# Eight raw weight tiles loaded into the empty ring of weights, and projections issued ahead of the sums of squares

## The chip, the cores and the metric

The kernel runs on one core of one Trainium2 chip. The metric is the device time of one execution in microseconds (us), the median of three runs. TensorE does the matmuls and loads their stationary operand ("weight load") by a part of its own; VectorE, ScalarE and GpSimd work on vectors, and SyncE issues the DMAs.

## The reference

Three stages follow one another, all in float32. Attention with random features (4 batches, 8 heads, 576 tokens, 64 numbers a head, 128 features):

```
phi(x) = exp(x_s @ omega.T - |x_s|^2/2 - max) / sqrt(128)     # x_s = x / 64**0.25
kv = phi(k).T @ v ;  z = sum of phi(k) over the tokens
attn = (phi(q) @ kv) / (phi(q) @ z + 1e-6)
```

Then a dense network on 2304 tokens of 512 numbers, `g = h if h > 0 else 0.01*h` with `h = x @ w_in` (512 x 2048) and `x1 = g @ w_out`; w_in and w_out come as 64-bit floats. Last, a gated network of eight experts: each token goes to the expert with the largest logit, through `relu(x1 @ w1[e]) @ w2[e]`, scaled by two gate values.

## The kernel before

The program is written in Python against a scheduler: it states operations in an order, and the scheduler lays them out in one fixed queue for each engine. An engine then runs its queue strictly in order and waits at an instruction until its operands and its destination are free.

**The opening.** The attention is cut into items of four 128-row tiles. A k item (27 of all) goes through the stages `s_load` (its inputs), `s_split` (squares of the inputs, line 270, on VectorE for the first three items, then on GpSimd), `s_proj` (the projection `pw` on omega, line 310, and the sums of squares `s2p`, line 288, as matmuls with `halves`), `s_phi` (the maximum `mx` on VectorE, line 322, then `ngm` and `bias`, lines 329 and 331, then four exponentials on ScalarE, line 339) and `s_kv` (the products `kvp` with v, line 379). A q item ends in transposes `qtp`, the product `nump` (line 441) and a transpose `xtp`, whose two halves `xh` and `xl` (line 216) are the input of the dense network. Thirteen items (k 0 to 7, the four of q that make the first 256 tokens, k 8) must be through before the first matmul `hp` of the dense network (lines 488 to 490), and three more begin before it; these sixteen take the sums of squares from TensorE (`by_pe`). `tick()` moves every open item one stage on.

In `project` the two matmuls for `s2p` stand ahead of those for `pw`, and VectorE copies `s2p` out of its bank at once (line 290).

**The weights.** `load_w` loads one half of a weight unit, 512 KB of 64-bit floats, into `wraw`, a ring of two tiles in the pool `wst`, and turns it into a pair of float32 tiles: ScalarE scales the upper word (line 205), VectorE puts the words together in three instructions (lines 206 to 208) into `w`, ScalarE copies to `wih` or `woh` (line 213) and GpSimd subtracts to `wil` or `wol` (line 216). Those pairs lie in `wring`, 32 tiles that the experts' weights use again later. Eight loads belong to the opening (`WPRE`), their order is `order`: w_in halves 0 and 1 of unit 0, w_out halves 0 and 1 of unit 0, then unit 1. A load is kept behind the newest input by `issue_after(newest[-1])`, and the third load waits until the first tile of the ring of two is free.

**The inputs.** The first nine k items come in three groups, `xgroup` and `vgroup`, loaded when the first item of a group begins; the others in pairs, `xpair`, a ring of three.

## Time and profile before

| | us |
|---|---|
| median of 3 runs | 829.49 |
| lowest, highest | 827.87, 835.15 |
| profiled execution, own time | 826.18 |
| its span, first to last instruction | 824.5 |
| TensorE busy in the span (matmul) | 805.0 (98%) |
| weight loads | 711.4 (86%) |
| VectorE, ScalarE, GpSimd | 438.6, 371.7, 152.0 |
| granted TensorE clock | 0.998 |

The profile is one execution. The page's slices show TensorE near full in all 40, and VectorE at 6 to 9 tenths in the first seven or so and at 3 to 6 later: the first tenth of the span is unlike the rest. Ends of matmuls are modelled, so that TensorE's gaps are better seen in the weight loads, whose idle time before each is listed with what ended it.

### The profile page before, as it was taken

How to read it: one execution, taken by the hardware profiler on the slowest of the kernel's cores; microseconds unless marked ns; L12 is line 12 of the kernel's file. 1: busy time of each engine (PE TensorE's matmuls, PEld its weight loads, DVE VectorE, ACT ScalarE, POOL GpSimd, SP SyncE). 2: the span in 40 equal slices, each digit the busy share in tenths (PEclk: the TensorE clock that was granted, in tenths of full speed). 3: DMA queues.
4: the chain of work that ended last, by engine and by line, in shares of the span. 5: the costliest groups of instructions: out<-in, count | busy, mean ns of one | idle time of the engine just before them, and what ended most of it. 6: DMA issues, size and time to landing. Idle time of an engine off the chain costs nothing. (4 is left out here: it accounts for less than half of the span.)

```text
span 824.5 us, 15807 instructions
## 1 busy us (share of the span) xinstructions
PE 805.0 (98%) x6037; PEld 711.4 (86%) x6037; DVE 438.6 (53%) x1118; ACT 371.7 (45%) x1238; POOL 152.0 (18%) x172
## 2 busy tenths in 40 slices
PE   9999999999999999999999999999999999999996
PEld 6777777788899898989898898888889989999994
DVE  6988779836644645634653544545644444343220
ACT  4887767625566236545425243122423434332210
POOL 3513324400211011121010010031004221130101
PEclk9999999999999999999999999999999999999999
DMA  6746655402342111152021000036306554150101
GB/s 217 217 126 178 197 172 166 151 8 71 81 84 73 45 20 52 58 71 64 26 32 21 2 26 1 27 110 102 78 28 209 165 167 144 56 162 27 45 14 35
DMA packets 45153, 72.74 MB, mean 88 GB/s; under 512 B 5905, under 2 KB 27665, under 8 KB 45074
## 3 DMA queue, kind: packets, MB, share of 16 engines
q1 hardware_dynamic: 41554, 62.22, 27.6%
q0 software_dynamic: 3520, 9.47, 3.7%
q8 instruction: 49, 0.80, 0.4%
q14 instruction: 30, 0.25, 0.1%
HBM read 61.08 MB, written 10.59 MB: 87 GB/s over the span
## 5 line engine op out<-in xcount | busy, mean ns | idle before, releaser
L488 PE MATMUL hp<-xh,wih 128*128 128x256 f32 x576 | 163.2, 283 | 0.9 <-ACT g L493 0.5
L490 PE MATMUL hp<-xh,wil 128*128 128x256 f32 x576 | 161.6, 281 | 2.3 <-POOL wil L216 2.2
L489 PE MATMUL hp<-xl,wih 128*128 128x256 f32 x576 | 161.6, 281 | 0.6 <-DVE xl L216 0.6
L508 PE MATMUL acc<-woh,gh 128*128 128x512 f32 x288 | 117.4, 408 | 0.8 <-ACT gh L213 0.8
L510 PE MATMUL acc<-woh,gl 128*128 128x512 f32 x288 | 114.7, 399 | 0.3 <-DVE gl L216 0.3
L509 PE MATMUL acc<-wol,gh 128*128 128x512 f32 x288 | 114.7, 398 | 0.0
L488 PEld LDWEIGHTS hp<-xh,wih 128*128 128x128 f32 x576 | 108.1, 188 | 3.8 <-ACT g L493 0.8
L490 PEld LDWEIGHTS hp<-xh,wil 128*128 128x128 f32 x576 | 108.1, 188 | 3.5 <-POOL wil L216 3.4
L489 PEld LDWEIGHTS hp<-xl,wih 128*128 128x128 f32 x576 | 108.1, 188 | 3.1 <-DVE xl L216 1.0
L495 DVE SCALAR_TENSOR_TENSOR g<-hp,g 128x512 f32<-128x512 f32 x56 | 38.6, 690 | 113.5 <-ACT g L493 113.0
L339 ACT ACTIVATE h<-pw,bias 128x128 f32<-128x128 f32 x288 | 84.9, 370 | 25.1 <-DVE bias L331 18.3
L493 ACT COPY g<-hp 128x512 f32<-128x512 f32 x72 | 42.2, 586 | 113.3 <-PE hp L490 113.3
L776 PE MATMUL eht<-exh,ewh 128*128 128x256 f32 (+1 forms) x256 | 76.5, 299 | 0.0
L778 PE MATMUL eht<-exh,ewl 128*128 128x256 f32 (+1 forms) x256 | 75.5, 295 | 0.0
L777 PE MATMUL eht<-exl,ewh 128*128 128x256 f32 (+1 forms) x256 | 75.4, 295 | 0.0
L281 ACT ACTIVATE nat<-nat 128x64 f32<-128x64 f32 x224 | 55.5, 257 | 40.6 <-DVE bias L331 27.8
L779 ACT ACTIVATE ehh<-eht 128x256 fp32r<-128x256 f32 (+1 forms) x64 | 26.4, 412 | 91.5 <-PE eht L778 91.3
L510 PEld LDWEIGHTS acc<-woh,gl 128*128 128x128 f32 x288 | 54.0, 188 | 13.1 <-DVE gl L216 1.0
L508 PEld LDWEIGHTS acc<-woh,gh 128*128 128x128 f32 x288 | 54.1, 188 | 11.5 <-ACT gh L213 1.6
L322 DVE TENSOR_REDUCE mx<-pw 128x4 f32<-128x512 f32 x66 | 45.2, 684 | 32.9 <-PE pw L305 22.2
L509 PEld LDWEIGHTS acc<-wol,gh 128*128 128x128 f32 x288 | 54.1, 188 | 9.6
L216 POOL TENSOR_TENSOR rawl<-xpair,rawh 128x256 fp32r<-128x256 f32 x38 | 29.4, 773 | 162.5 <-ACT rawh L213 153.6
(176 smaller groups left out, 1636.5 us busy)
## 6 DMA issues: line engine op xcount, KB each, us to landing
eraw<-w SPq DMA_DIRECT2D x32, 512.0 KB, 3.7
wraw<-w_in SPq DMA_DIRECT2D x16, 512.0 KB, 3.9
wraw<-w_out SPq DMA_DIRECT2D x16, 512.0 KB, 3.7
x_d<-rows SPq DMA_DIRECT2D x9, 514.0 KB, 3.4
xpair<-qT SPq DMA_DIRECT2D x18, 256.0 KB, 3.1
nat<-k_nat SPq DMA_DIRECT2D x27, 128.0 KB, 3.0
xpair<-kT SPq DMA_DIRECT2D x12, 256.0 KB, 2.7
nat<-q_nat SPq DMA_DIRECT2D x23, 128.0 KB, 2.2
```

The source lines that it names most:

```text
L281: nc.scalar.activation(nat[:, j], nat[:, j], AF.Square, scale=math.sqrt(sc * sc / 2.0), accum_out=s2[:, j:j + 1])
L322: nc.vector.tensor_reduce(o, pj.rearrange("p (j h) m -> p j h m", h=2), axis=AX.X, op=ALU.max)
L339: st["e_last"] = nc.scalar.activation(h[:, j, :], src[:, j // 2, j % 2], AF.Exp, bias=bias[:, j:j + 1], scale=sc).ins
L488: nc.tensor.matmul(hp[:, i, :], a, xh[:, d, :], start=d == 0, stop=False)
L489: nc.tensor.matmul(hp[:, i, :], a, xl[:, d, :], start=False, stop=False)
L490: nc.tensor.matmul(hp[:, i, :], b_, xh[:, d, :], start=False, stop=d == ND - 1)
L508: nc.tensor.matmul(acc[t], a, h_, start=u == 0 and i == 0, stop=False)
L509: nc.tensor.matmul(acc[t], a, l_, start=False, stop=False)
L510: nc.tensor.matmul(acc[t], b_, h_, start=False, stop=u == NU - 1 and i == 1)
L776: nc.tensor.matmul(t, wh, self.xh[:, d, 0:n], start=d == 0, stop=False)
L777: nc.tensor.matmul(t, wh, self.xl[:, d, 0:n], start=False, stop=False)
L778: nc.tensor.matmul(t, wl, self.xh[:, d, 0:n], start=False, stop=d == ND - 1)
```

## The change

Eight tiles of the still empty `wring` serve as raw tiles for the eight loads of the opening, so that none of these waits for the ring of two. The three k groups are loaded first, in one go (`k_group`), then two raw tiles, and each further raw tile after a `load_w` (`ahead`); in the opening they are no longer tied behind the newest input. In `project` the projections now stand ahead of the sums of squares, `s2p` stays in its bank, and VectorE copies it in `phi`, behind the maximum. The squares `sq` get a third place (the tag `g`). All other work is the same: each engine has as many instructions of each kind as before, and the queues are equal again from about the 1,050th of TensorE's 5,751 instructions on.

```diff
+        spare = [wring.tile([P, 512, 2], I32, name="wraw", tag="w") for _ in range(WPRE)]
+        raws = {}
+
+        def raw_of(kind, u, half, raw):
+            with ExitStack() as order_:
+                if dense[0]:
+                    order_.enter_context(tc.issue_after(newest[-1]))
+                if kind == "in":
+                    nc.sync.dma_start(raw.rearrange("p (i a) b -> p i (a b)", i=2),
+                                      w_in[2 * half * P:2 * (half + 1) * P, u * 256:(u + 1) * 256].bitcast(I32).rearrange("(i p) a -> p i a", i=2))
+                else:
+                    f = 2 * u + half
+                    nc.sync.dma_start(raw.rearrange("p a b -> p (a b)"), w_out[f * P:(f + 1) * P, :].bitcast(I32))
+            return raw
...
-            raw = pool.tile([P, 512, 2], I32, name="wraw", tag="wraw")
+            if (kind, u, half) not in raws:
+                raws[kind, u, half] = raw_of(kind, u, half, pool.tile([P, 512, 2], I32, name="wraw", tag="wraw"))
+            raw = raws.pop((kind, u, half))
...
-                with tc.issue_after(newest[-1]):
...
+        def fetch(dst, src):
+            newest.append(nc.sync.dma_start(dst, src).ins)
+
+        def group_of(src, at, grp):
 
             first, m, big = grp
-            if at == first:
+            if (src.tensor.name, first) not in groups:
...
-                sq = sb.tile([P, 2 * P], F32, name="sq", tag="gl")
+                sq = sb.tile([P, 2 * P], F32, name="sq", tag="g" if st["turn"] % 3 == 2 else "gl", bufs=1 if st["turn"] % 3 == 2 else 2)
...
         def project(st, nt):
-            if st["by_pe"]:
-                s2 = ps_h.tile([P, 2, 2], F32, name="s2p", tag="h")
-                for j in range(2):
-                    nc.tensor.matmul(s2[:, j, :], st["sq"][:, j * P:(j + 1) * P], halves, start=True, stop=True)
-                s2s = att.tile([P, 4], F32, name="s2", tag="s2")
-                nc.vector.tensor_copy(s2s.rearrange("p (h j) -> p j h", h=2), s2)
-                st["s2"] = s2s
...
             st["pj"] = pj
+            if st["by_pe"]:
+                s2 = ps_h.tile([P, 2, 2], F32, name="s2p", tag="h")
+                for j in range(2):
+                    nc.tensor.matmul(s2[:, j, :], st["sq"][:, j * P:(j + 1) * P], halves, start=True, stop=True)
+                st["s2"] = s2
...
             s2 = st["s2"]
+            if st["by_pe"]:
+                s2 = att.tile([P, 4], F32, name="s2", tag="s2")
+                nc.vector.tensor_copy(s2.rearrange("p (h j) -> p j h", h=2), st["s2"])
...
+        def k_group(first, m):
+            group_of(kT, first, (first, m, True))
+            vs = sb.tile([P, 1024], F32, name="vgroup", tag="xl", bufs=3)
+            vs = vs[:, 0:m * 5 * HV].rearrange("p (m n) -> p m n", m=m)
+            fetch(vs, v_nat[first:first + m].rearrange("m p n -> p m n"))
+            groups["v", first] = vs
...
+        def ahead():
+            if spare:
+                o = order[WPRE - len(spare)]
+                raws[o] = raw_of(*o, spare.pop(0))
+
+        for at in range(0, 9, 3):
+            k_group(at, 3)
+        ahead()
+        ahead()
         for i in range(first + LEAD):
             tick(seq.pop(0) if i < first + NEW else None)
             while loaded < min(WPRE, (i - WFROM) * WPRE // (first + LEAD - WFROM)):
                 load_w(*order[loaded], wst)
                 loaded += 1
+                ahead()
 
 
         tabv = tab_d.rearrange("(c n) o -> c (n o)", n=SLOT)
```

TensorE's queue at the first k items, before. `s2p` are the sums of squares, `pw` the projections, `kvp` the products with v:

```order
L288 MATMUL s2p<-halves,sq 128x2 x2
L310 MATMUL pw<-om_raw,xgroup 128x256 x2
L288 MATMUL s2p<-halves,sq 128x2 x2
L310 MATMUL pw<-om_raw,xgroup 128x256 x2
L288 MATMUL s2p<-halves,sq 128x2 x2
L310 MATMUL pw<-om_raw,xgroup 128x256 x3
L379 MATMUL kvp<-vgroup,h 64x132 x2
L379 MATMUL kvp<-vgroup,h 64x66 x2
L310 MATMUL pw<-om_raw,xgroup 128x256
L379 MATMUL kvp<-vgroup,h 64x66 x4
L288 MATMUL s2p<-halves,sq 128x2 x2
L379 MATMUL kvp<-vgroup,h 64x66 x4
```

and after the change:

```order
L317 MATMUL pw<-om_raw,xgroup 128x256 x2
L322 MATMUL s2p<-halves,sq 128x2 x2
L317 MATMUL pw<-om_raw,xgroup 128x256 x2
L322 MATMUL s2p<-halves,sq 128x2 x2
L317 MATMUL pw<-om_raw,xgroup 128x256 x2
L322 MATMUL s2p<-halves,sq 128x2 x2
L317 MATMUL pw<-om_raw,xgroup 128x256
L396 MATMUL kvp<-vgroup,h 64x132 x2
L396 MATMUL kvp<-vgroup,h 64x66 x2
L317 MATMUL pw<-om_raw,xgroup 128x256
L396 MATMUL kvp<-vgroup,h 64x66 x4
L322 MATMUL s2p<-halves,sq 128x2 x2
```

The projection of an item now stands first, and the sums of squares come to lie between a projection and the products with v; the last item's first half of a projection still meets `kvp` directly.

VectorE's queue around the first weight conversion, before (`w_187` is the first converted tile, `mx` the maximum of one item):

```order
L322 TENSOR_REDUCE mx<-pw 128x2x2
L206 TENSOR_SCALAR w_187<-w_187 128x512
L290 COPY s_303<-s2p 128x2x2
L207 SCALAR_TENSOR_TENSOR w_187<-wraw,w_187 128x512
L329 SCALAR_TENSOR_TENSOR ngm<-mx,s_267 128x4
L322 TENSOR_REDUCE mx<-pw 128x2x2
L208 SCALAR_TENSOR_TENSOR w_187<-wraw,w_187 128x512
L206 TENSOR_SCALAR w_255<-w_255 128x512
L331 TENSOR_TENSOR bias<-ngm,s_267 128x4
```

and after (`w_197` is the first converted tile):

```order
L346 TENSOR_TENSOR bias<-ngm,s_354 128x4
L334 TENSOR_REDUCE mx<-pw 128x2x2
L217 TENSOR_SCALAR w_197<-w_197 128x512
L342 COPY s_387<-s2p 128x2x2
L218 SCALAR_TENSOR_TENSOR w_197<-wraw,w_197 128x512
L344 SCALAR_TENSOR_TENSOR ngm<-mx,s_387 128x4
L334 TENSOR_REDUCE mx<-pw 128x2x2
L219 SCALAR_TENSOR_TENSOR w_197<-wraw,w_197 128x512
L217 TENSOR_SCALAR w_264<-w_264 128x512
L346 TENSOR_TENSOR bias<-ngm,s_387 128x4
```

The first conversion stood behind the fifth `mx` and now stands behind the seventh, and the copy out of `s2p` stands behind the maximum of its item.

SyncE's queue of DMA issues, before, from the second k group on:

```order
L250 DMA xgroup<-kT 128x3x256
L352 DMA vgroup<-v_nat 128x3x330
L188 DMA wraw<-w_in 128x2x512 x2
L250 DMA xgroup<-kT 128x3x256
L352 DMA vgroup<-v_nat 128x3x330
L250 DMA xpair<-qT 128x2x256
L200 DMA wraw<-w_out 128x1024
L250 DMA xpair<-qT 128x2x256
L200 DMA wraw<-w_out 128x1024
L250 DMA xpair<-qT 128x2x256 x2
```

and after:

```order
L251 DMA xgroup<-kT 128x3x256
L251 DMA vgroup<-v_nat 128x3x330
L251 DMA xgroup<-kT 128x3x256
L251 DMA vgroup<-v_nat 128x3x330
L183 DMA wraw<-w_in 128x2x512 x2
L251 DMA xpair<-qT 128x2x256 x3
L251 DMA nat<-q_nat 128x256
L251 DMA nat<-k_nat 128x256
L381 DMA vb<-v_nat 128x330
L381 DMA vb<-v_nat 128x264
L187 DMA wraw<-w_out 128x1024 x2
```

The third k group and its v went ahead of the two w_in tiles, three pairs of q follow without a w_out load between them, and w_out comes behind those and small loads of later items.

## Rows read from the trace of the kernel before

**Rows 1.** Busy us per engine (x instructions), clock, DMA share, GB/s; two stages.

```profile
0.00:46.50 46.50, 43.79 (x380) 32.96 (x380) 36.28 (x109) 29.39 (x85) 19.05 (x32) 1.00 0.65 206
...
165.00:230.00 65.00, 64.41 (x502) 56.90 (x501) 35.02 (x114) 30.86 (x121) 8.20 (x10) 1.00 0.21 52
```

**Rows 2.** Timeline of weight loads: start, length, what, count, [idle before, releaser].

```profile
4.36 0.93 PEld L288 LDWEIGHTS s2p<-halves,sq 128*128 128x128 f32 x4 [0.54 <-PE warm L143]
...
6.72 0.73 PEld L310 LDWEIGHTS pw<-om_raw,xgroup 128*128 128x128 f32 x4
...
16.52 0.55 PEld L379 LDWEIGHTS kvp<-vgroup,h 128*64 128x64 f32 x16 [0.33 <-issue]
17.14 0.30 PEld L310 LDWEIGHTS pw<-om_raw,xgroup 128*128 128x128 f32 x2
17.46 0.63 PEld L288 LDWEIGHTS s2p<-halves,sq 128*128 128x128 f32 x4
18.01 0.30 PEld L310 LDWEIGHTS pw<-om_raw,xgroup 128*128 128x128 f32 x2
...
22.89 0.52 PEld L288 LDWEIGHTS s2p<-halves,sq 128*128 128x128 f32 x4
23.42 0.31 PEld L379 LDWEIGHTS kvp<-vgroup,h 128*64 128x64 f32 x8
```

**Rows 3.** Weight loads by group, 0 to 46.5 us: busy, mean ns, idle before.

```profile
L379 PEld LDWEIGHTS kvp<-vgroup,h 128*64 128x64 f32 x144 | 6.3, 136 | 3.7 <-ACT h L339 2.0 <-issue 1.0 <-ACT woh L213 0.3
...
L441 PEld LDWEIGHTS nump<-kv,et 128*64 128x64 f32 x64 | 2.2, 137 | 1.2 <-ACT et L430 0.3 <-ACT wih L213 0.3 <-ACT h L339 0.3
```

**Rows 4.** The same timeline of weight loads, later.

```profile
21.43 0.52 PEld L288 LDWEIGHTS s2p<-halves,sq 128*128 128x128 f32 x4 [0.45 <-POOL sq L270]
...
34.47 1.16 PEld L310 LDWEIGHTS pw<-om_raw,xpair 128*128 128x128 f32 x6 [1.23 <-DMA xpair<-kT]
...
49.94 0.19 PEld L489 LDWEIGHTS hp<-xl,wih 128*128 128x128 f32 x1 [1.02 <-DVE xl L216]
```

**Rows 5.** Timeline of VectorE (DVE), same columns.

```profile
6.59 0.69 DVE L322 TENSOR_REDUCE mx<-pw 128x4 f32<-128x512 f32 x1 [0.68 <-PE pw L310]
...
15.00 0.42 DVE L206 TENSOR_SCALAR w<-w 128x512 int32<-128x512 int32 x1
...
15.74 0.69 DVE L207 SCALAR_TENSOR_TENSOR w<-wraw,w 128x512 int32<-128x512 int32 x1
...
17.44 0.67 DVE L208 SCALAR_TENSOR_TENSOR w<-wraw,w 128x512 int32<-128x512 int32 x1
...
19.24 1.67 DVE L208 SCALAR_TENSOR_TENSOR w<-wraw,w 128x512 int32<-128x512 int32 x1
...
24.28 0.68 DVE L322 TENSOR_REDUCE mx<-pw 128x4 f32<-128x512 f32 x1
...
37.57 0.16 DVE L443 TENSOR_SCALAR rec<-nump 128x4 f32<-128x4 f32 x1 [1.25 <-PE nump L441]
...
49.48 0.41 DVE L216 TENSOR_TENSOR xl<-xtp,xh 128x256 fp32r<-128x256 f32 x1
```

**Rows 6.** Timeline of ScalarE (ACT).

```profile
8.98 3.21 ACT L339 ACTIVATE h<-pw,bias 128x128 f32<-128x128 f32 x12 [6.68 <-DVE ngm L329]
```

**Rows 7.** VectorE by group, 15 to 49.9 us: busy, mean ns, idle before.

```profile
L207 DVE SCALAR_TENSOR_TENSOR w<-wraw,w 128x512 int32<-128x512 int32 x8 | 7.3, 916 | 0.0
L208 DVE SCALAR_TENSOR_TENSOR w<-wraw,w 128x512 int32<-128x512 int32 x8 | 6.4, 802 | 0.0
```

**Rows 8.** Timeline of GpSimd (POOL).

```profile
18.85 1.50 POOL L216 TENSOR_TENSOR wil<-w,wih 128x512 fp32r<-128x512 f32 x1 [1.95 <-ACT wih L213]
```

**Rows 9.** Timeline of the DMA issues on SyncE.

```profile
18.19 0.34 SPq L200 DMA_DIRECT2D wraw<-w_out  x1
...
54.69 0.89 SPq L188 DMA_DIRECT2D wraw<-w_in  x2
```

**Rows 10.** Longest TensorE wait, 46 to 230 us: total, times, longest.

```profile
PE hp L490 <- POOL wil L216: 2.2, 3, 1.1
```

More of the change, by code (lines that the diff above doesn't have):

```diff
@@ L186, in load_w @@
                 wh, wl = win[u]
-                with tc.issue_after(newest[-1]):
-                    nc.sync.dma_start(raw.rearrange("p (i a) b -> p i (a b)", i=2),
-                                      w_in[2 * half * P:2 * (half + 1) * P, u * 256:(u + 1) * 256].bitcast(I32).rearrange("(i p) a -> p i a", i=2))
                 wh, wl = wh[:, 2 * half:2 * half + 2, :], wl[:, 2 * half:2 * half + 2, :]
@@ L197, in load_w @@
                 wh, wl = wout[u]
-                f = 2 * u + half
-                with tc.issue_after(newest[-1]):
-                    nc.sync.dma_start(raw.rearrange("p a b -> p (a b)"), w_out[f * P:(f + 1) * P, :].bitcast(I32))
                 wh, wl = wh[:, half, :], wl[:, half, :]
@@ L237, in xt_tiles @@
             return xT[c]
-        def group_of(st, src, at, grp):
+        def fetch(dst, src):
+            newest.append(nc.sync.dma_start(dst, src).ins)
+        def group_of(src, at, grp):
             first, m, big = grp
-            if at == first:
+            if (src.tensor.name, first) not in groups:
                 if big:
@@ L249, in group_of @@
                 for a, b in zip(cuts, cuts[1:]):
-                    newest.append(nc.sync.dma_start(t[:, a:b], src[at + a:at + b].rearrange("m p c -> p m c")).ins)
+                    fetch(t[:, a:b], src[at + a:at + b].rearrange("m p c -> p m c"))
                 groups[src.tensor.name, first] = t
@@ L255, in split_x @@
             st["turn"] = next(turns)
-            st["raw"] = group_of(st, src, at, grp)
+            st["raw"] = group_of(src, at, grp)
             st["tight"] = not both_done[0]
@@ L263, in split_x @@
                 st["nat"] = att.tile([P, 4, HD], F32, name="nat", tag="nat")
-                newest.append(nc.sync.dma_start(st["nat"][:, 0:nt, :], nat).ins)
+                fetch(st["nat"][:, 0:nt, :], nat)
         def squares(st, nt):
             if st["by_pe"]:
-                sq = sb.tile([P, 2 * P], F32, name="sq", tag="gl")
+                sq = sb.tile([P, 2 * P], F32, name="sq", tag="g" if st["turn"] % 3 == 2 else "gl", bufs=1 if st["turn"] % 3 == 2 else 2)
                 (nc.vector if st["turn"] < 3 else nc.gpsimd).tensor_mul(sq, st["raw"], st["raw"])
@@ L347, in s_load @@
             def s_load():
-                split_x(st, kT, 9 * b + g, grp, k_nat[b, g], 4)
-                if big and at == first:
-                    vs = sb.tile([P, 1024], F32, name="vgroup", tag="xl", bufs=3)
-                    vs = vs[:, 0:m * 5 * HV].rearrange("p (m n) -> p m n", m=m)
-                    nc.sync.dma_start(vs, v_nat[at:at + m].rearrange("m p n -> p m n"))
-                    groups["v", first] = vs
+                split_x(st, kT, at, grp, k_nat[b, g], 4)
             def s_split():
```

## The prediction, made before the changed kernel ran

> **What bounds the kernel now.** I read the stages first. From 165 us on TensorE is busy 64.41 of 65.00 us, and in the first 46.5 us 43.79 [rows 1]. The queues of before and after are the same from about TensorE's 1,050th instruction on, so all that the change can give or cost lies in the opening and the 100 us behind it. The next view is the timeline of weight loads, which shows TensorE's gaps better than the matmuls, whose ends are modelled. A float32 matmul is two instructions there: a whole projection is four loads.
>
> Three things are to be seen in it. First, TensorE really is close to full in the opening: behind the warm-up its first real load comes at 4.36 [rows 2], and most loads follow one another at once. Second, a gap of 0.33 us stands ahead of `kvp` behind a projection, and it is put down to "issue" (nothing that the profile shows) as well as to ScalarE [rows 2, 3]. Behind `s2p` there is none: 22.89 + 0.52 = 23.41, and `kvp` starts at 23.42 [rows 2]. A gap that has the same length whoever is named is not a wait for data; it goes with the pair of neighbours. Third, TensorE can't start the dense network fully before 49.94, where `hp` waits for `xl`, the last half of the fourth q item, which VectorE writes at 49.48 [rows 4, 5].
>
> So two engines share the opening: TensorE, and from 15.00, when the first conversion starts, VectorE, whose queue ends in that `xl`. What VectorE does there I read from its timeline. The longest hole in it behind 15.00 is 1.25 us at 37.57, where it waits for TensorE's `nump` [rows 5].
>
> **The change, part by part.** Nothing is added to or taken from any engine's count. The extra raw tiles cost no instruction. They take places 0 to 7 of the ring of 32; the weights of units 0 to 5 take the next 24, and those of units 6 and 7 take the eight raw places again, long after their conversion. Cost: 0. The work that hides their allocation is the same 24 pairs' conversion; were it late, unit 6 would wait for it.
>
> *Projection first.* Before, the first maximum waits until 6.59 for a projection that stood behind `s2p` [rows 5]. Now the projection's loads begin at 4.36. One `s2p` is 18.01 - 17.46 = 0.55 [rows 2], so `mx` moves to about 5.8 to 6.0. ScalarE's first exponentials at 8.98 [rows 6] follow; since `bias` still stands behind the second `mx`, I take 0.6 of those 0.8 for TensorE's first `kvp`.
>
> *Fewer gaps.* All gaps ahead of `kvp` and `nump` in the opening come to 3.7 + 1.2 = 4.9 us [rows 3], which is about fourteen of 0.33. In the new queue I count seven places where `kvp` or `nump` still follows a projection or a transpose directly (three around the first three k items, four among the q items). Seven times 0.33 is 2.3 us saved.
>
> *Waits in the middle.* `s2p` waited 0.45 for squares from GpSimd, which had two places; with three and with squares ahead of the weight splits in its queue I count that as gone. A projection waited 1.23 for a pair from memory [rows 4]. That pair still needs a place in the ring of three, so the issue moves with the projection that frees it; I take half, 0.6.
>
> TensorE's own sum is 0.6 + 2.3 + 0.45 + 0.6 = 3.9 us. It is not the answer, because VectorE must follow.
>
> *VectorE.* The first conversion now stands behind the seventh `mx`. When is that? From the first load at 4.36: three rounds of projection and sums of squares of 0.75 + 0.55 each (the projection is 0.73 and a start-up of 0.02 [rows 2]) end at 8.26. Half a projection ahead of `kvp` is 0.32 (17.14 to 17.46) plus the gap of 0.33; a whole `kvp` is 17.14 - 16.52 = 0.62, with the change of tile 0.7, a half 0.39. The queue from there is half `pw`, half `kvp`, half `pw`, half `kvp`, `s2p`, half `kvp`, half `pw`, half `kvp`, half `pw`, `s2p`, `kvp`, `pw`, `s2p`, `kvp`, `pw`: the gap stands three times, 4 x 0.32 + 3 x 0.33 + 4 x 0.39 + 3 x 0.55 + 2 x 0.7 + 2 x 0.75 = 8.4, and the seventh projection is loaded at 16.6 and through at 17.0 (the stream behind the last load put at the gap of 0.33 and a little). With `mx` of 0.69 the first conversion starts at 17.6, against 15.00 before [rows 5]: 2.6 later.
>
> From there two conversions and the eighth and ninth `mx` remain up to a point that both queues share. so 2 x (0.33 + 0.61 + 0.61) + 2 x 0.61 + 0.6 of small ones + 0.2 of waiting for the eighth projection = 5.1, which is 22.7; I add 1.0 for one collision with GpSimd of the size of 19.24 (1.67 against 0.67 [rows 5]) and have 23.7. Before, the ninth `mx` started at 24.28 and ended at 24.96 [rows 5] with the same two conversions done. VectorE is 1.3 us ahead. From there to the last `xl` its work is the same in both, and its longest hole, 1.25 for `nump`, closes because TensorE is further ahead. Together 1.3 + 1.2 = 2.5 us: `xl` ends at 47.4 and not at 49.89. What is late next is again VectorE; TensorE waits 1 us or more for `xl`, and 3.9 - 2.5 = 1.4 of its own gain is lost there.
>
> *The loads.* The third weight tile was issued at 18.19, when the ring of two came free [rows 9]; now it is issued without that wait. But its conversion stands in the queues of ScalarE and VectorE behind the first two, so an earlier arrival alone gives nothing: cover is VectorE's queue from 17.6 on; without it the gain would be bounded by that same 2.5. The loads of unit 2 were issued at 54.69 behind two `nat` loads [rows 9], and in the new queue they still stand behind two `nat` loads. I count 0 for everything after 50 us.
>
> Bounds. From below: the 2.6 that the conversion starts later is not won back at all, and TensorE's gain is used up by it; that is 0. From above: TensorE's 3.9 in full and a further 0.6 of the DMA wait, 4.5. I take 2.5, the value from VectorE's rows, since that engine ends last.
>
> **Rule and row.** The second and third passes of a conversion read two tiles from SBUF. One of them took 1.67 at 19.24 while GpSimd ran a split of 1.50 from 18.85, against 0.67 alone [rows 5, 8]; over the sixteen passes the means are 916 and 802 ns against 0.69 and 0.67 alone, which is 8 x 0.23 + 8 x 0.13 = 2.9 us [rows 5, 7]. The Trainium skill (SBUF — State Buffer, "Who interferes with whom") says that VectorE with two SBUF inputs and a GpSimd instruction that reads SBUF exclude each other for a whole instruction, whichever comes first. The trace agrees at 19.24. It speaks against the change: conversions are packed into a shorter stretch together with the same eight splits. By the rule alone the sum would be that of the second rival below, 832.1; by the row, which counts the stretch already paid, 827.0.
>
> **The rivals.**
> - *Nothing moves.* VectorE is the bound, starts its conversions 2.6 later and only just makes it up. For it: VectorE is busy 36.28 of 46.5, with most of its room ahead of 15.00. Against it: the 1.3 counted above. Time 826.2 in the profile, 829.5 as a median.
> - *The shared port.* Each of the eight splits stops one pass for 1.0: 8.0 in place of 2.9, so 5.1 lost against 2.5 won, 2.6 slower: 832.1. It needs every split to hit; before, about three did.
> - *Sums of squares hold a bank* (the slower one). `s2p` shares two banks with `qtp`, `nump`, `xtp` and `hp`, and is now read only behind the maximum. If TensorE reaches the next of those tiles before the copy, it waits one maximum, 0.68, and with a conversion pass between, 1.36. Eight items lie in the q part: 5.4 to 10.9 lost, 2.5 won, so 2.9 to 8.4 slower: 832.4 to 837.9. It decides as soon as VectorE runs more than one item behind TensorE; the queue shows such pairs near the end of the opening, where VectorE is late anyway.
> - *More is won.* Conversions that end earlier also end the waits of `hp` for GpSimd's splits, 2.2 of 7.4 us in eleven groups between 46 and 230 us [rows 10]: 4.7 with these alone, 9.9 with all. Middle 6.5: 823.0. Against it: the loads of unit 2 start as late as before.
>
> **How the numbers follow.** The profiled execution took 826.18 us, and 826.18 - 2.5 = 823.7. The median of the runs, 829.49, stands 3.3 above it, so the predicted median is 829.5 - 2.5 = 827.0. Chances: forecast (1 to 4.5 won) 0.50, nothing moves 0.20, shared port 0.08, bank 0.10, more won 0.12. The forecast's own range is 825.0 to 828.5. The range takes in the neighbours up to 832.4 above, where the bank's cheaper end lies, and 821.5 below, a little under the middle of the last case; the dearer bank and the last waits are left out. A measurement can tell 1%, 8.3 us, from no change: faster by that needs nearly all of 9.9, 0.05; slower needs the dear end of the bank, 0.03; the rest, 0.92, is within.
>
> **What would show it.** Right: the first exponentials at 8.0 to 8.5; no gaps of 0.33 ahead of `kvp` behind `s2p`; the first conversion pass at 17 to 18; the last `xl` of the opening at 47 to 48; `hp` full from there. Wrong: `xl` at 49.5 or later (nothing moves); passes of 1.2 to 1.7 us eight times (port); gaps ahead of `qtp`, `nump` or `xtp` put down to the copy of `s2p` (bank); waits for splits between 60 and 110 us gone (more won).

## The result, and the profile of the changed kernel

| | before | changed |
|---|---|---|
| median of 16 runs, us | 828.75 | 835.65 |
| lowest, highest | 826.96, 835.15 | 834.42, 837.61 |
| profiled execution, us | 826.18 | 834.47 |
| its span | 824.5 | 832.7 |

The ratio is 1.0081, 95% interval 1.0067 to 1.0096: 0.8% slower, 6.9 us, where 827.0 was forecast (821.5 to 832.4). The kernel that came best out of the experiments is the same change with the old order of the queues; it is 1.9 us faster than before (0.9977, 0.996 to 0.9993), which is only just clear of no change.

Up to 24 us the changed kernel runs close to the forecast's times. VectorE's timeline (start, length, engine, line, operation, operands, count, [idle before, releaser]) answers to [rows 5]:

```profile
5.48 0.68 DVE L334 TENSOR_REDUCE mx<-pw 128x4 f32<-128x512 f32 x1
...
17.68 0.74 DVE L217 TENSOR_SCALAR w<-w 128x512 int32<-128x512 int32 x1
...
22.90 1.24 DVE L219 SCALAR_TENSOR_TENSOR w<-wraw,w 128x512 int32<-128x512 int32 x1
...
29.83 0.68 DVE L219 SCALAR_TENSOR_TENSOR w<-wraw,w 128x512 int32<-128x512 int32 x1
30.42 0.42 DVE L217 TENSOR_SCALAR w<-w 128x512 int32<-128x512 int32 x1
30.76 0.15 DVE L342 COPY s<-s2p 128x4 f32<-128x4 f32 x1
...
52.29 0.41 DVE L227 TENSOR_TENSOR xl<-xtp,xh 128x256 fp32r<-128x256 f32 x1
```

The first maximum is 1.11 us earlier than before, the first conversion starts at 17.68 (forecast 17.6), and two conversions and the ninth maximum are done at 24.14 (forecast 23.7, before 24.96). Some of this early lead is luck. TensorE's first matmuls ran fast at once in some executions and slowly in others, also with the same queues: the first four of `pw` took 1.03 us in this execution and 1.69 in that of s1 (an experiment below), whose queues are the same up to there, and in the kernel before the first four of `s2p` took 0.85 and the next ones 0.50. s1, with the slow start like the kernel before, is 0.87 later from the second maximum on (the ninth is at 23.17 against 22.30). The changed kernel, then s1:

```profile
4.30 1.03 PE L317 MATMUL pw<-om_raw,xgroup 128*128 128x256 f32 x4
```

```profile
4.52 1.69 PE L325 MATMUL pw<-om_raw,xgroup 128*128 128x256 f32 x4
...
23.77 1.23 DVE L227 SCALAR_TENSOR_TENSOR w<-wraw,w 128x512 int32<-128x512 int32 x1
```

With like starts VectorE is therefore done with two conversions and nine maxima at 25.00 (s1), which is where the kernel before was (24.96).

Then a copy of `s2p` stands behind passes of two different conversions, at 30.76, and the last `xl` of the opening starts at 52.29 and ends at 52.70, where 47.4 was forecast. What TensorE does meanwhile stands in the timeline of weight loads, which answers to [rows 2, 4]:

```profile
24.81 0.52 PEld L322 LDWEIGHTS s2p<-halves,sq 128*128 128x128 f32 x4 [0.59 <-POOL sq L284]
...
31.03 0.42 PEld L445 LDWEIGHTS qtp<-ident,h 128*128 128x128 f32 x4 [2.08 <-issue]
...
42.72 0.52 PEld L322 LDWEIGHTS s2p<-halves,sq 128*128 128x128 f32 x4 [1.10 <-POOL wil L227]
44.80 0.74 PEld L322 LDWEIGHTS s2p<-halves,sq 128*128 128x128 f32 x4 [1.43 <-POOL wil L227]
45.42 1.40 PEld L317 LDWEIGHTS pw<-om_raw,xpair 128*128 128x128 f32 x4
...
49.40 0.19 PEld L505 LDWEIGHTS hp<-xh,wih 128*128 128x128 f32 x1
...
52.75 0.19 PEld L506 LDWEIGHTS hp<-xl,wih 128*128 128x128 f32 x1 [1.27 <-DVE xl L227]
...
91.20 0.19 PEld L525 LDWEIGHTS acc<-woh,gh 128*128 128x128 f32 x1 [1.93 <-ACT kv L415]
...
119.36 0.30 PEld L317 LDWEIGHTS pw<-om_raw,xpair 128*128 128x128 f32 x2 [2.55 <-ACT kv L415]
```

The pause of 2.08 us is named "issue" here; the matmul's own row, in the timeline of TensorE, names the copy:

```profile
31.06 0.63 PE L445 MATMUL qtp<-ident,h 128*128 128x128 f32 x4 [1.71 <-DVE s L342]
...
42.75 0.58 PE L322 MATMUL s2p<-halves,sq 128*128 128x2 f32 x4 [0.99 <-DVE rec L460]
...
44.83 0.80 PE L322 MATMUL s2p<-halves,sq 128*128 128x2 f32 x4 [1.22 <-DVE xl L227]
```

The pauses of 1.10 and 1.43 ahead of `s2p` are not GpSimd's either: its splits `wil` had ended at 41.72 and 44.26. The matmuls' rows name VectorE's `rec` and `xl`, and `xl` of 42.19 stands directly behind a conversion pass of 1.42 us.

By group, 0 to 49.4 us, the gaps have moved (busy, mean ns, idle before; answers to [rows 3]):

```profile
L322 PEld LDWEIGHTS s2p<-halves,sq 128*128 128x128 f32 x64 | 9.4, 195 | 4.1 <-POOL wil L227 2.9 <-POOL sq L284 0.6
...
L396 PEld LDWEIGHTS kvp<-vgroup,h 128*64 128x64 f32 x144 | 5.7, 136 | 1.3 <-ACT h L354 0.7 <-issue 0.5
L445 PEld LDWEIGHTS qtp<-ident,h 128*128 128x128 f32 x20 | 2.8, 163 | 2.6 <-issue 2.3
L458 PEld LDWEIGHTS nump<-kv,et 128*64 128x64 f32 x64 | 2.2, 137 | 1.4 <-ACT xh L224 0.9 <-PE qtp L445 0.3 <-issue 0.2
```

`kvp` and `nump` have 2.7 us of idle time ahead of them, where before it was 4.9; `s2p` and `qtp` have 6.7, where before they had 2.3 (1.7 and 0.6).

And the granted clock falls to half, 1.2 of 2.4 GHz, in three stretches, each of which begins behind such pauses. (The pause of 2.08 at 31.03 brought no fall in this execution.) The stages by windows (columns as in [rows 1]; the number behind the engines is the clock):

```profile
0.00:49.40 49.40, 42.82 (x380) 33.76 (x380) 39.03 (x113) 29.73 (x85) 18.41 (x32) 0.97 0.61 197
...
45.03:48.44 3.41, 3.36 (x12) 2.49 (x11) 1.97 (x6) 1.16 (x5) 0.00 (x0) 0.50 0.00 0
92.82:96.23 3.41, 3.20 (x8) 2.52 (x9) 2.68 (x7) 3.17 (x15) 0.21 (x1) 0.50 0.52 180
120.12:123.53 3.41, 3.41 (x9) 2.61 (x10) 3.27 (x7) 1.31 (x2) 0.00 (x0) 0.50 0.45 162
```

Before, the clock is 1.00 up to the last 5 us. At half clock the projection's four loads at 45.42 took 1.40 us; at full clock such four took 0.73 [rows 2]. The profiled execution had a mean clock of 0.992; twelve of the sixteen runs had 0.986 to 0.989, so most spent more time at half clock than the three stretches. Their times hardly show it: they average 835.9 us, and the four at 0.992 to 0.994 average 835.0.

Where the 8.3 us of span went: the first `hp` is 2.9 later (49.40 against 46.51), the next 144 loads of `hp` take 56.2 us and not 52.4, the 432 behind those 148.2 and not 149.0, and all the rest, where the queues are equal again, 2.4 more. Other pairs of profiles differ there by up to 6 us, so that only the first two differences are read here. With like starts the first may be larger, by up to the 0.87 above.

### The profile page after: what moved, and what is told of

Read it like the earlier page. It is cut to its first block, busy times and chain, and to the rows that moved or that the text cites. A ratio compares the mean times of both kernels' runs of the same rounds, so it can differ in the third digit from the quotient of the medians.

```text
span 832.7 us, 15803 instructions
## 1 busy us (share of the span) xinstructions
PE 805.6 (97%) x6037; PEld 713.6 (86%) x6037; DVE 440.3 (53%) x1118; ACT 371.2 (45%) x1238; POOL 150.2 (18%) x172
## 4 chain that ended last, share of the span: by engine, by line
PE 69%; issue 11%; DVE 9%; DMA 6%; ACT 3%; POOL 1%; SPq 0%; POOLq 0%; ACTq 0%; DVEq 0%
PE acc L525 7%; PE acc L527 7%; PE acc L526 7%; PE hp L505 6%; PE hp L506 6%; PE hp L507 6%; PE eht L803 2%; PE pw L317 2%; PE eht L805 2%; PE eht L804 2%; PE nump L458 2%; DMA eraw<-w 2%; PE kvp L396 2%; DVE w L219 2%; PE qtp L445 2%
## 5 line engine op out<-in xcount | busy, mean ns | idle before, releaser
L295 ACT ACTIVATE nat<-nat 128x64 f32<-128x64 f32 x224 | 55.7, 257 | 42.4 <-DVE bias L346 27.3
L527 PEld LDWEIGHTS acc<-woh,gl 128*128 128x128 f32 x288 | 54.9, 191 | 13.3 <-DVE gl L227 0.4
L525 PEld LDWEIGHTS acc<-woh,gh 128*128 128x128 f32 x288 | 54.7, 190 | 13.0 <-ACT kv L415 1.9
L526 PEld LDWEIGHTS acc<-wol,gh 128*128 128x128 f32 x288 | 54.7, 190 | 9.5
```

The source lines that it names most:

```text
L295: nc.scalar.activation(nat[:, j], nat[:, j], AF.Square, scale=math.sqrt(sc * sc / 2.0), accum_out=s2[:, j:j + 1])
L525: nc.tensor.matmul(acc[t], a, h_, start=u == 0 and i == 0, stop=False)
L526: nc.tensor.matmul(acc[t], a, l_, start=False, stop=False)
L527: nc.tensor.matmul(acc[t], b_, h_, start=False, stop=u == NU - 1 and i == 1)
```

## The experiments

All times are device time; a ratio is to the kernel before on the same chip, and a difference in us (+4.6) is what the ratio makes of 829 us. In the table, "hp" is the start of the first `hp` load and "half clock" lists the stretches at 1.2 GHz up to 200 us, start and length, both of the one profiled execution. That execution was the slowest of its kernel's runs in f1, f2, f3, s2, p1 and p4, 2.9 to 6.0 us above the median, so their traces show a bad case.

| run | median us | ratio, 95% | hp | half clock |
|---|---|---|---|---|
| e1_order_only | 832.59 | 1.0056 (1.003, 1.0081) | 48.4 | none |
| e2_loads_only | 835.41 | 1.0086 (1.0054, 1.0118) | 50.1 | 46.5 (3.4) |
| e3_copy_at_once | 833.72 | 1.0077 (1.0049, 1.0105) | 53.0 | 26.3 (6.8), 50.2 (3.4) |
| e4_hold_only | 830.98 | 1.0036 (1.0022, 1.0051) | 49.8 | none |
| p1_loads_kept_queues | 828.75 | 0.9991 (0.9972, 1.0011) | 46.8 | none |
| p3_hold_kept_queues | 831.81 | 1.0025 (1.0005, 1.0044) | 48.7 | none |
| p5_after_queues_old_loads | 837.22 | 1.0072 (1.0051, 1.0094) | 52.3 | 31.2 (6.8), 48.3 (3.4) |
| p6_change_kept_queues | 828.38 | 0.9977 (0.996, 0.9993) | 45.9 | none |
| q1_after_pe_queue_alone | 848.16 | 1.0238 (1.0214, 1.0262) | 47.6 | four |
| q2_loads_swap_copy_at_once | 829.57 | 1.0016 (1.0003, 1.0029) | 48.2 | none |
| p4_swap_hold_kept_queues | 828.89 | 1.0005 (0.9989, 1.0021) | 50.1 | 36.8 (3.4) |
| p2_swap_kept_queues | 832.37 | 1.0043 (1.0023, 1.0062) | 51.5 | 33.0 (6.8) |
| s1_after_order_to_22us | 830.78 | 1.0037 (1.0023, 1.005) | 49.7 | 29.7 (3.4) |
| s2_after_order_22_to_50us | 833.48 | 1.0063 (1.0045, 1.0081) | 51.9 | 31.4 (6.8), 48.5 (6.8) |
| s3_after_order_from_50us | 832.88 | 1.0054 (1.0036, 1.0071) | 49.5 | 29.7, 118.4 (3.4 each) |
| f1_raw_tiles_behind_first_group | 829.81 | 1.0029 (1.0014, 1.0043) | 48.5 | 44.6, 102.6, 119.7 (3.4 each) |
| f3_copies_first_in_after_order | 832.05 | 1.0043 (1.003, 1.0057) | 49.3 | 48.1, 119.8, 150.5 (3.4 each) |
| f2_kept_queues_early_raw | 834.49 | 1.0064 (1.0038, 1.0089) | 59.2 | 13.3 (27.3) |

### Halves of the change, the scheduler free

e1 puts the change's `project`, its copy behind `mx` and its third place for `sq` into the kernel before; e4 only the copy:

```diff
-                s2s = att.tile([P, 4], F32, name="s2", tag="s2")
-                nc.vector.tensor_copy(s2s.rearrange("p (h j) -> p j h", h=2), s2)
-                st["s2"] = s2s
+                st["s2"] = s2
...
             s2 = st["s2"]
+            if st["by_pe"]:
+                s2 = att.tile([P, 4], F32, name="s2", tag="s2")
+                nc.vector.tensor_copy(s2.rearrange("p (h j) -> p j h", h=2), st["s2"])
```

e2 undoes just that in the changed kernel (its loads stay), and e3 leaves the change whole but for the copy, which again stands directly behind the two matmuls of `s2p`.

> The kernel before with one half of the change: projections ahead of the sums of squares, the copy of s2p behind the maximum, the third place for squares; the loads of k groups and weights as before. Bank theory (s2p held in one of two banks until its copy behind the maximum makes TensorE wait for qtp, nump, xtp and the next s2p, and the pauses lower the clock): slower than before by 4 to 8 us, pauses of 1 to 2 us put down to VectorE's copy between 25 and 46 us, and at least one stretch at the lower clock. Load theory (the eight early loads push the conversions into a shorter and later stretch): within 2 us of before, no such pauses.

> The changed kernel with the other half alone: the eight raw tiles in the empty ring and the k groups loaded first; sums of squares ahead of the projection and copied at once, two places for squares, as before the change. Bank theory: within 2 us of before (827 to 831), no pause of TensorE over 1 us put down to the copy of s2p. Load theory: slower than before by 4 to 8 us.

> The changed kernel with one edit: VectorE copies s2p right behind the sums of squares (ahead of the maximum), so that the bank comes free early; projections still first, loads as in the change. Bank theory: the loss goes, 825 to 830, the pauses of 1 to 2 us at 28 to 45 us shrink below 0.5, no low clock before 60 us. Load theory: still 834 to 837.

> The kernel before with one edit: s2p stays in its bank and is copied behind the maximum of its item; sums of squares still ahead of the projection, loads as before. Bank theory: slower by 4 to 8 us, as in the change. Load theory: within 2 us of before. A theory by which only the order projection first matters (sums of squares late): within 2 us of before as well.

Measured: +4.6, +7.1, +6.4 and +3.0 us. Each half costs by itself, the halves add up to more than the whole, and e3 shows that the copy at once heals nothing. So neither theory held. What the four have in common is that the scheduler laid all queues anew: e4 moves sixteen small copies, and in its trace 725 of TensorE's 6,037 matmul places and 288 of ScalarE's 1,238 hold another instruction than before.

### The same edits, the queues held

A table of places pins an engine's queue; nothing waits for it, it only fixes which instruction follows which:

```diff
+QUEUES = {"PE": [(0, 8), ...], "Activation": [...], "DVE": [...], "Pool": [...]}
...
+        for e, stretches in QUEUES.items():
+            queue = [made[e][k] for a, n in stretches for k in range(a, a + n)]
+            for one, two in zip(queue, queue[1:]):
+                tc.add_manual_dep(two, one.name, mybir.DependencyInfo(mybir.DependencyClass.NoSync, mybir.DependencyReason.DATA), reason="queue")
```

p1 is e2 with the four queues of the kernel before. p3 is e4 with them, only the copies moved. p6 is the changed kernel with them, where only the matmuls of `s2p` (behind their projection) and the copies (behind their maximum) have moved; one item of the sixteen keeps its old place (behind its projection two tiles would wait for each other's bank: read from the program, not run). p5 is e1 with the four queues of the changed kernel. SyncE's queue was not held: of its 214 places in the trace, 19, 12 and 21 differ from the kernel before in p1, p3 and p6, and 8 from the changed kernel in p5.

> The loads of the change alone (k groups first, eight spare raw tiles, no tie to the newest input), while the queues of TensorE, ScalarE, VectorE and GpSimd are held word for word in the order of the kernel before. Theory A (what costs is the new order that the scheduler lays out, not the loads or the held bank themselves): within 2 us of the kernel before, first hp at 46 to 47 us. Theory B (held bank): within 2 us as well. Theory C (the early loads themselves, as the run with the loads alone suggested with its 7.7 us): 5 to 9 us slower, first hp at 49 to 51.

> Only the sixteen copies of s2p are moved behind the maximum of their item in VectorE's queue; all other instructions of the four engines stand in the order of the kernel before. Theory A (new order): within 2 us, first hp at 46 to 48. Theory B (held bank, which cost 3.3 us when the scheduler was free to re-lay the rest): 3 to 6 us slower, with gaps of TensorE ahead of qtp, nump, xtp or s2p put down to that copy. Theory C (loads): within 2 us.

> The four engines' queues are those of the changed kernel word for word, but the weights come through the ring of two and the inputs are loaded group by group as before. Theory A (new order): as slow as the changed kernel or slower, 6 to 10 us over the kernel before, since conversions can only start later than there. Theory B (held bank): 4 to 8 us over. Theory C (loads): within 2 us of the kernel before.

> The whole change (loads, third place for squares, sums of squares behind the projection for fifteen of the sixteen items, copy behind the maximum), but each engine's queue is otherwise the one of the kernel before: only the sums of squares and their copies have moved. Theory A (new order): faster by 0 to 3 us, first hp at 44 to 47. Theory B (held bank): 3 to 6 us slower. Theory C (loads): 5 to 9 us slower.

Theory C (the loads) falls with p1: the same loads that cost 7.1 us in e2 cost nothing (-0.7, interval -2.3 to +0.9). Theory B (the bank) is left with 2.1 us in p3 (0.4 to 3.6). Theory A stands: the whole change is 1.9 us faster than before once the queues are kept, and p5 has the changed kernel's loss without its loads. The difference between p6 and the changed kernel, one program in two orders, is 0.0104 of 829, 8.6 us. Weight loads and VectorE of p6:

```profile
30.70 0.31 PEld L453 LDWEIGHTS qtp<-ident,h 128*128 128x128 f32 x3 [1.08 <-ACT woh L232]
...
45.87 0.19 PEld L513 LDWEIGHTS hp<-xh,wih 128*128 128x128 f32 x1 [0.21 <-DVE s L350]
```

```profile
5.79 0.68 DVE L342 TENSOR_REDUCE mx<-pw 128x4 f32<-128x512 f32 x1
...
14.12 0.43 DVE L225 TENSOR_SCALAR w<-w 128x512 int32<-128x512 int32 x1 [0.69 <-ACT w L224]
...
48.10 0.41 DVE L235 TENSOR_TENSOR xl<-xtp,xh 128x256 fp32r<-128x256 f32 x1
```

No pause of 2 us, first `hp` 0.6 earlier than before, last `xl` 1.4 earlier than in [rows 5]. p6's execution had the quick start and that of the kernel before the slow one, worth about 0.9 us at first, so the gain rests on the medians and not on these two rows. Against the changed kernel, which had the quick start too, the first `hp` of p6 is 3.5 us earlier.

### Which part of the change gives, and TensorE's order alone

q1 is the changed kernel with TensorE's queue as changed and the other three as in p6. q2 is e3 in p6's order, with the copies at their old places; p4 is p6 without the loads and without the third place for squares; p2 moves only the matmuls of `s2p`.

```diff
 # p2, project(): the two matmuls and the copy behind the projection
             st["pj"] = pj
+            if st["by_pe"]:
+                s2 = ps_h.tile([P, 2, 2], F32, name="s2p", tag="h")
+                ...
+                nc.vector.tensor_copy(s2s.rearrange("p (h j) -> p j h", h=2), s2)
```

> The changed kernel, with TensorE's queue word for word the changed one, but ScalarE's, VectorE's and GpSimd's queues in the order of the kernel before (the copies of s2p behind their maxima). Theory V (what costs is the new order on VectorE and ScalarE, where weight conversions stand in pairs, back to back, ahead of the copy of s2p and of the chain rec, xr, xl): within 2 us of the kernel before, first hp at 45 to 47, no qtp gap of 2 us near 31. Theory P (TensorE's new order itself): 5 to 8 us slower, as the changed kernel, first hp at 49 or later. The held bank alone would make it 2 us slower, by the run with the held copies.

> The loads of the change and the projection first for fifteen of sixteen items, with the queues of the kernel before and with the copy of s2p at its old place in VectorE's queue (before the maximum). If the held bank costs the 2 us that the run with the held copies showed: 3 to 5 us faster than the kernel before, first hp at 43.5 to 45.5. If the held bank costs only where the order is bad otherwise: the same as the change with kept queues, 1 to 3 us faster.

> Projection first for fifteen of sixteen items and the copy behind the maximum, with the queues of the kernel before, but with the loads and the two places for squares of the kernel before. If the loads give nothing (as with the loads alone): 0 to 3 us faster than the kernel before, the same as the whole change with kept queues. If it is the loads, or the third place for squares, that bring the gain once the projections run earlier: within 1 us of the kernel before or up to 2 slower, with waits of the conversions for the ring of two.

> Only the sums of squares moved behind the projection in TensorE's queue for fifteen of sixteen items; every other queue is as before and s2p is copied at its old place. By the forecast's own terms for TensorE (gaps of 0.33 us that go where sums of squares stand between a projection and the products): 1 to 3 us faster, first hp at 44.5 to 46. If VectorE alone sets the end of the opening: within 1 us.

q1 was to tell V from P and tells neither: +19.7 us is outside both. A queue of one engine is worth little without those that it was laid with. Of the other three only p4 came out as one of its theories had it (within 1 us: the gain needs the loads or the third place for squares as well, though its interval just meets that of p6). Together they show how the parts hang together: projection first alone is 3.6 us slower, with the copy behind the maximum 0.4 slower, with both and the loads 1.9 faster; with the loads but the copy at its old place, 1.3 slower. VectorE's timeline shows one reason. In p2 the old copy waits for an `s2p` that now comes later, and the maximum stands behind it:

```profile
6.51 0.16 DVE L318 COPY s<-s2p 128x4 f32<-128x4 f32 x1 [1.39 <-PE s2p L316]
...
6.92 0.68 DVE L330 TENSOR_REDUCE mx<-pw 128x4 f32<-128x512 f32 x1
```

In p4 the copy stands behind the maximum, but with two places for squares the third square, ahead of the maximum too, waits for the same `s2p`:

```profile
6.72 0.42 DVE L278 TENSOR_TENSOR sq<-xgroup 128x256 f32<-128x256 f32 x1 [1.10 <-PE s2p L316]
7.06 0.69 DVE L328 TENSOR_REDUCE mx<-pw 128x4 f32<-128x512 f32 x1
```

Only the copy behind the maximum, which the bank rival counted as a loss, together with the third place for squares lets the first maximum follow the projection: it is at 5.79 in p6, at 6.92 in p2 and at 7.06 both in p4 and in q2 (third place, but the copy at its old place). The start explains part of that as well (quick in p6, slow in p2, p4 and q2; s1, slow, with copy and third place as in the change, has 6.24). That this first maximum makes the whole difference between the four runs is not shown.

### Where in the new order the loss is made

s1, s2 and s3 are the changed kernel with one stretch of its own order and p6's order in the other two (cut behind the second conversion, about 22 us, and at the first `hp`); only the table differs. f1 leaves the scheduler free and moves two loads:

```diff
-        for at in range(0, 9, 3):
-            k_group(at, 3)
+        k_group(0, 3)
         ahead()
         ahead()
+        k_group(3, 3)
+        k_group(6, 3)
```

f3 is the changed kernel in its own order, with the copies of `s2p` pulled directly behind their maxima in VectorE's table. f2 is p6 with f1's loads.

> The changed kernel in the order that the scheduler gave it up to the end of the second weight conversion (about 22 us), and from there in the kept order of the kernel before. If the loss lies in the order of 22 to 50 us or later: as fast as the change with kept queues or faster, 1 to 4 us under the kernel before. If it is the late first conversion (17.7 against 14.1 us): 3 to 8 us over the kernel before.

> The kept order up to the second conversion, the scheduler's order of the changed kernel from there to the first hp (about 22 to 50 us), the kept order behind it. If the loss is made in the middle stretch, where four conversion passes stand ahead of one copy of s2p: 3 to 8 us slower than the kernel before, with a gap of 1.5 us or more ahead of a qtp. If it is made before or after: 2 us faster to 1 us slower.

> The kept order up to the first hp, the scheduler's order of the changed kernel from there on. If the waits of 1.9 and 2.6 us for the copies of kv near 91 and 119 us come from the order there: 2 to 5 us slower than the kernel before. If they only pass on a delay from the opening: 2 us faster to 1 us slower.

> The changed kernel with one edit: the first two raw tiles are loaded behind the first k group and not behind all three; the scheduler is free. It lays the first conversion behind the third maximum (not the seventh) and spreads the first four conversions. If the late and paired conversions are what costs: 4 to 9 us faster than the changed kernel, so within 3 us of the kernel before either way. If the new order is bad for other reasons: within 3 us of the changed kernel, 4 to 9 us over the kernel before.

> The changed kernel, all queues word for word, but the sixteen copies of s2p are pulled directly behind their maxima in VectorE's queue; the one behind qtp's 2.08 us gap then runs at about 29.9 and not at 30.76. If the held bank makes the loss: that gap falls to about 1.1 us, and the kernel is 2 to 5 us faster than the changed one, so 2 to 5 us over the kernel before. If the copies' place matters little beside the order of everything else: within 1.5 us of the changed kernel, 5 to 8 us over the kernel before.

> The change with kept queues, and the first two raw tiles loaded behind the first k group and not behind all three. With kept queues ScalarE waited 2.4 us for the first raw tile before it began the first conversion; if that sets the rest, the first conversion starts at 13 and not at 14.1, first hp at 44.5 to 45.5, 2 to 4 us faster than the kernel before. If the other k groups come too late instead: within 1 us of the kernel before or slower, with waits for an xgroup.

s2, the middle stretch alone, has most of the loss, 5.2 us over before, and the changed kernel's pauses at the same places (2.36, 1.09, 1.43 against 2.08, 1.10, 1.43). Its first conversion starts at 14.4, as early as in p6, so the late first conversion is not needed for the loss; its third stands behind the eleventh maximum (27.67, as in the changed kernel) and not behind the ninth (23.41 in p6):

```profile
31.04 0.42 PEld L453 LDWEIGHTS qtp<-ident,h 128*128 128x128 f32 x4 [2.36 <-issue]
...
45.69 0.52 PEld L330 LDWEIGHTS s2p<-halves,sq 128*128 128x128 f32 x4 [1.09 <-POOL wil L235]
47.77 0.52 PEld L330 LDWEIGHTS s2p<-halves,sq 128*128 128x128 f32 x4 [1.43 <-POOL wil L235]
```

s1 and s3 can't be read by their totals. Both have a seam at the cut near 22 us: ScalarE's scaling of the third weight tile lies behind it, later than in p6, while VectorE's queue asks for it as early as there. In s3 that made a hole of 2.42 us in VectorE, and TensorE waited 3.26 us for exponentials behind it; s1 has the same hole (1.18) and a wait of 3.87, and s2 has none there:

```profile
25.64 1.03 DVE L225 TENSOR_SCALAR w<-w 128x512 int32<-128x512 int32 x1 [2.42 <-ACT w L224]
```

What s3 does show is its stretch behind 50 us. With the changed order there, the waits for the copies of kv come back, at 91.11 and 117.97; s2, with p6's order there, has 0.82 at 119.60:

```profile
91.11 0.19 PEld L533 LDWEIGHTS acc<-woh,gh 128*128 128x128 f32 x1 [1.34 <-ACT kv L423]
...
117.97 0.30 PEld L325 LDWEIGHTS pw<-om_raw,xpair 128*128 128x128 f32 x2 [2.40 <-ACT kv L423]
```

The 144 loads of `hp` there take 54.7 us in s3 and 52.1 in p6. f1 wins back 4.3 us of the loss (1.0081 to 1.0029): with the raw tiles behind the first k group the scheduler puts the first conversion behind the third maximum and the third behind the seventh, and takes the first four apart. f3 wins back 3.1 (1.0081 to 1.0043) by the place of the copies alone, as its bank case had it; the pause of 2.08 us is 1.29 there, at 31.87. The two overlap, and were not tried together. f2 came out on the slow side, with the wait for an `xgroup` that its second case named. In the profiled execution TensorE waited 2.27 us for the second k group, and from 13.3 us on the clock stayed at half for 27.3 us, though TensorE was busy:

```profile
11.66 0.30 PEld L325 LDWEIGHTS pw<-om_raw,xgroup 128*128 128x128 f32 x2 [2.27 <-DMA xgroup<-kT]
```

```profile
13.00:41.00 28.00, 28.00 (x170) 23.19 (x169) 14.63 (x38) 10.27 (x33) 9.67 (x11) 0.51 0.45 136
```

That was its slowest run, 840.44 us at a mean clock of 0.982. Its two runs at 0.993 took 830.2 and 830.3, about 2 over the kernel before, so most of its loss goes with the clock.

## Why the prediction was wrong, point by point

- **Projection first**: right in size. `mx` at 5.48 (forecast 5.8 to 6.0) and ScalarE's first exponentials at 7.54 (8.0 to 8.5) are earlier than forecast by the luck of a quick start; s1, with the slow start of the kernel before, has its exponentials at 8.41, 0.57 ahead of 8.98, where 0.6 was counted.
- **Fewer gaps**: right. 4.9 - 2.7 = 2.2 us saved ahead of `kvp` and `nump`, forecast 2.3.
- **VectorE, up to the ninth maximum**: 24.14 for 23.7 looks right, but only by the quick start. With like starts it is 25.00 (s1) against 24.96 before: the lead of 1.3 us in the sum was none.
- **VectorE, from there on**: this step failed. "From there to the last xl its work is the same in both" is true of the work and not of its order. From the third on the conversions stand later among the items (behind the eleventh maximum and not the ninth), and the copy of `s2p`, on which a bank hangs, and the chain from `nump` to `xl` stand between and behind their passes. The forecast had `xl` end 2.5 us earlier; it ended 2.8 later, and TensorE's three longest pauses of the opening wait for the copy, `rec` and `xl`. That the order of this stretch by itself makes the loss is shown by s2, that the program without it gains by p6 (-1.9, interval -3.3 to -0.6; the forecast was -2.5). So the sum was made for the old queue with the edit in it, and not for the queue that ran. That p6's 1.9 comes near the 2.5 is no proof of its terms, since the lead of 1.3 was not there.
- **Loads: 0**. Right as a direct cost (p1). But where the raw tiles stand among the loads is what led the scheduler to the late conversions: f1 moves only that and wins back 4.3 us.
- **Everything after 50 us: 0**. Wrong. The first 144 `hp` loads lost 3.8 us, with two waits for the copies of kv and two stretches at half clock. That the order behind 50 us brings such waits is shown by s3; why ScalarE is late there was not followed.
- **The bank rival** had a chance of 0.10 and deserved more. It decided where it said, with VectorE more than one item behind: one wait of 1.71 us and some smaller ones, not eight of 0.68 to 1.36. Its part in the changed order is about 3.1 us (f3). Its price in the old order is 2.1 alone (p3), and a gain once the projection goes first (p6 against q2, 3.2 us).
- **The shared port** fell: the passes of [rows 7] now take 7.3 + 5.5 = 12.8 us together and not 13.7 (rows below). Four of the sixteen passes were longer than 0.7 us, and each ran beside GpSimd, two of them beside a split (1.24 at 22.90, split of 1.27 from 22.32; 1.42 at 40.84, split of 1.53 from 40.18), and not eight of 1.2 to 1.7. The rule of the Trainium skill (SBUF — State Buffer, "Who interferes with whom"), by which two such instructions exclude each other, is borne out by these passes.
- **More is won**: the middle of 4.7 and 9.9 is 7.3 and not 6.5; the forecast does not rest on it.
- **The clock** was no term of the forecast at all. The three stretches hold 10.0 us of busy TensorE at half speed; were all of it bound by the clock, they would cost about 5 us, an estimate from above: the sixteen runs (0.9 us between those at a higher and a lower clock) show no such price.

VectorE by group in the changed kernel, 17.6 to 52.8 us:

```profile
L219 DVE SCALAR_TENSOR_TENSOR w<-wraw,w 128x512 int32<-128x512 int32 x8 | 7.3, 909 | 0.0
L218 DVE SCALAR_TENSOR_TENSOR w<-wraw,w 128x512 int32<-128x512 int32 x8 | 5.5, 688 | 0.0
```

Open is how the 8.6 us split between the late conversions, the copies, the order behind 50 us and the clock: every mixed order (q1, s1 to s3) was 3 to 20 us slower than the kernel before, so that the parts could not be added.

## What to carry to other kernels

Where a scheduler lays the queues, an edit of sixteen small instructions can re-lay several hundred, and the edit's own effect (here 1.9 us faster) may be smaller than that of the new order (here 8.6 slower). Read the new queue to its end, not only around the edit: look for what a freed or held bank stands behind on the slower engine, and for long passes that now stand later among the items. To learn what an edit itself is worth, hold the queues of the old kernel and move only what the edit means to move. And before a lead of 1 us between two traces is read, compare how fast their first instructions ran.

## What the runs showed of the hardware

Short pauses of TensorE could cost twice, their own time and a lower clock behind them. No pause in these openings was longer than 3.9 us, most were 1 to 2.4, and still the granted clock fell to 1.2 GHz behind some of them: for 3.41 us behind pauses of 1.10 and 1.43 (changed kernel), for 6.83 behind one of 2.36 (s2), for 27.3 behind one of 2.27 (f2), with TensorE busy in between. Pauses of 1.35 (e1) and 1.08 (p6) brought none. The length of the pause does not decide it: the changed kernel and p5 have the same four queues and the same pause of 2.08 us ahead of `qtp` (at 31.03 and 31.12), and the clock stayed at full speed behind the first and fell for 6.83 us, from 31.22, behind the second. In e3 it fell for 6.83 us, from 26.27, behind a pause of 0.97. What else decides was not followed. The clock can also spread the runs of one kernel: of p5's ten, the two at a mean clock of 0.994 took 832.4 and 833.2 us, the eight at 0.987 to 0.990 836.9 to 838.9. The changed kernel's sixteen show no such spread (834.8 at 0.994, 834.4 at 0.987).
